# Linear attention and maxout feed-forward on one core: q^T of batch 2 by the DMA crossbar instead of TensorE, batch 3's loads behind it

## Chip, cores and metric

One core of one Trainium2 chip. The metric is the device time of the whole kernel in microseconds (us); the time of a kernel is the median of its runs. Engines are called PE (TensorE), ACT (ScalarE), DVE (VectorE), POOL (GpSimd) and SP (SyncE).

## What is computed

q, k and v have 8 batches, 8 heads, 1024 positions and 64 features. E and F (64 x 1024) shorten k and v along the positions; then a softmax over the 64 shortened positions, and a feed-forward layer with a maximum of two branches. In float32:

```python
k_proj = einsum('ks,bhsd->bhkd', E, k)
v_proj = einsum('ks,bhsd->bhkd', F, v)
scores = matmul(q, k_proj.transpose(0, 1, 3, 2)) / sqrt(64)
attn = softmax(scores)
x = matmul(attn, v_proj)                  # heads side by side: [8192, 512]
out = maximum(x @ w1, x @ w2) @ w_out     # w1, w2: 512 x 1024, w_out: 1024 x 512
```

## The kernel before

Everything runs on one core, with fp16 operands and float32 sums, as one list of steps whose order is written out by hand (`manual_schedule`). Each engine executes its own instructions in the order in which they were written; waits between engines are semaphores, and so are waits for DMAs.

Loads. q, k and v of a batch come in whole, one DMA of 1 MB (fp16) for each tensor, issued from POOL's queue (`load`, L101-105), into tiles of one pool with four buffers (`kvq`, L46): a load waits until the tile of four allocations before it is read. Outputs are stored from SP's queue (`store`, L646-652), from a pool of four buffers (`opool`).

Attention of a batch. `step_kv` (L172) projects k and v, `step_kpt` (L207, on PE) or `step_kpt_dma` (L222, on SP's queue) transposes the projected k, and q has to be transposed too, since the scores contract over the features. There are two ways to do that in the file:

- `step_qt` (L232-245): for four heads and two position blocks, 8 PE transposes of 128 x 128 (L237, matmuls with the identity) into a PSUM bank, then one DVE copy of 128 x 1024 from PSUM into the tile `qt` (L242). Four calls make the q^T of a batch. Batches 0, 1 and 2 use it.
- `step_qt_dma` (L248-252): two DMA transposes from the loaded q tile straight into `qt`, four heads each, issued from SP's queue. Batches 3 to 7 use it.

`step_gate` (L228) is a 1 x 1 copy on POOL that reads the tile named, so that POOL's queue stands still until that tile has been written; the loads of the next batch are written behind it. Batches 3 to 7 have such a gate on `kpt` (L852), and behind it the loads of batch b + 1, as long as there is one.

`step_group` (L333) computes the scores of four heads and half the positions (`score`, L266) and, in the same stretch, the sums and values of the group before (L278). There are four groups to a batch.

Feed-forward. The positions of a batch are cut into two units (batch, half), 16 in all. `up_steps` (L535, matmuls at L554) makes the hidden layer of a unit and `down_steps` (L606, matmuls at L632) its output, both as seven products of half-size blocks, Strassen style, with sums on DVE (L515, L569, L572, L656) and copies on ACT (L525, L604, L700).

Order. The list `slots` (L775-793) strings up the work of unit n: pieces of its down products, with the up products of unit n + 1 between them, in two halves h. Its keys are `("P", n, p, i)` for the pieces of unit 0, `("G", n, h)` for the place where a group of scores goes, `("U", n, h, i)` for up step i. `at_slot` hangs a step behind a key. Batch b's preparation hangs on unit 2b - 3 (L838-853): batch 2 on unit 1, batch 3 on unit 3. For batch 2 the order before is: `step_kv` and the loads of q and v of batch 3 at `("G", 1, 0)`, `step_kpt` at `("U", 1, 0, 1)`, and the four calls of `step_qt` at `("U", 1, 0, 0)`, `("U", 1, 0, 3)`, `("U", 1, 0, 5)` and `("U", 1, 1, 5)`. The first scores of batch 2 stand at `("G", 1, 1)` and use heads 0 to 3; heads 4 to 7 are first read at `("G", 2, 0)`. The load of k of batch 3 stands earlier, with the last `step_qt` of batch 1 (L831).

Which k comes when is decided in `loads` (L756-760): for small b it loads the k of the batch after.

Of the kernel before, what the change touches and what calls it, by code (L numbers as in the profile page):

```python
# [16 lines left out]
def kernel(  # L17
# [14 lines left out]
    B, H, S, D = q.shape  # L32
# [33 lines left out]
    def att_banks(dtype=FP32):  # L66
# [9 lines left out]
            name=nc.get_next_instruction_name(),  # L76
# [20 lines left out]
    def load_all(t, b, n, src):  # L97
        alloc(t, n)
        load(t, n, src, b, 0, H)
# [352 lines left out]
    U = {(b, o): {"n": n, "b": b, "o": o, "t": tiles[b]} for n, (b, o) in enumerate(units)}  # L452
# [260 lines left out]
    t = tiles[0]  # L713
# [41 lines left out]

    def loads(b, *names):  # L756
        for n in names:
            b_ = b + (n == "k" and b < 3)
            if b_ < B:
                load_all(tiles[b_], b_, n, {"k": k, "v": v, "q": q}[n])  # L760

    slots = [
        (0, u0[0]), (None, f(step_at, 0, 1)), (1, u0[1]), (None, f(step_at, 1, 1)),
        (None, lambda: loads(1, "v", "q", "k")),
        (None, wd[1]), (2, u1[0]), (3, u1[1]), (4, u0[2]), (None, wt[0]), (5, u0[3]),
        (None, wd[2]), (None, wt[1]), (6, u1[2]), (7, u1[3]), (8, u0[4]), (9, u0[5]), (None, wd[3]),
# [30 lines left out]
    def at_slot(key, s, *a):  # L797
        steps.setdefault(key, []).append(lambda: s(*a))
# [11 lines left out]
    t = tiles[1]  # L810
    at_slot((0, 19), new_attn, t)
    at_slot((0, 19), lambda: turn.__setitem__(slice(None), [2, 3]))
    for n, x in enumerate((
        "kv", "", "kpt", "qt00 qt10", "", "sc00 qt01 qt11", "sc10", "dn00 in00", "sc01",
        "at00 dn10 in10", "sc11", "at10 dn01 in01", "dn11 in11", "at01", "at11",
    )):
        key = ("P", 0, (n - 1) // 2, (n - 1) % 2) if n else (0, 19)
        for name in x.split():
            if name[0] == "k":
                if name == "kpt":  # L820
                    at_slot(key, step_kpt, t, 0, H, True)
                else:
                    at_slot(key, step_kv, t)
                    at_slot(key, loads, 2, "v", "q")
            else:
                g, j = int(name[2]), int(name[3])
                s_ = {"qt": step_qt, "sc": step_sc,
                      "dn": step_dn, "in": step_inv, "at": step_at}[name[:2]]
                at_slot(key, s_, t, *((4 * g, 4, 2 * j, 2 * j + 2) if name[:2] == "qt" else (g, j)))
                if name == "qt11":  # L830
                    at_slot(key, loads, 2, "k")  # L831
        if n in (1, 5):
            at_slot(key, step_t, 1, (0, 1) if n == 1 else (2, 3))
        if 6 <= n < 10:
            at_slot(key, sums_x, U[0, 1], ((2, 0, 1, 3)[n - 6],))


    t = tiles[2]  # L838
    at_slot(("P", 0, 6, 0), new_attn, t)
    at_slot(("G", 1, 0), step_kv, t, 0, H, "kv", True)  # L840
    at_slot(("G", 1, 0), loads, 3, "q", "v")
    at_slot(("U", 1, 0, 1), step_kpt, t, 0, H, True)
    for i, key in enumerate((("U", 1, 0, 0), ("U", 1, 0, 3), ("U", 1, 0, 5), ("U", 1, 1, 5))):
        at_slot(key, step_qt, t, 4 * (i % 2), 4, i // 2 * 2, i // 2 * 2 + 2, True)
    for b in range(3, B):
        t = tiles[b]
        n = 2 * b - 3
# [8 lines left out]
    for i, (new, old) in enumerate(zip([*groups, none], [none, *groups])):  # L856
        n, h = divmod(i + 3, 2)
# [64 lines left out]
```

## Time and profile before

| | |
|---|---|
| median of 4 runs | 335.63 us (335.35 to 336.16) |
| the profiled execution, its time | 335.29 us |
| its span in the profile | 333.5 us |
| so outside the span | 1.79 us |
| PE busy | 321.5 us (96%) |
| DVE busy | 242.2 us (73%) |
| ACT busy | 201.6 us (60%) |
| granted PE clock, mean | 0.994 |
| unit 1, from its first down piece to its last up step | about 70.3 to 91.6 us in the span |

How to read it: the profile shows one execution, with times in us from the start of its span. A group of instructions is a line of the kernel with its engine, operation and operands, with the busy time, the mean of one, and the idle time of the engine ahead of it. The chain of work that ended last is followed back from the last instruction, at each step to what released it, or else to the instruction before it on its engine: what stands on the chain sets the end of the run, what doesn't stand there lies beside other work. A DMA's time to landing runs from its issue to the semaphore that says its data are there. The time for which an instruction of SP is shown is the time for which it holds SP's queue; the transfer itself goes on after it.

### The profile page before, as it was taken

The numbers are of one execution on the slowest core, as the hardware profiler recorded it, in microseconds if no ns is written. First come the engines' busy times: TensorE is split into PE (matmuls) and PEld (weight loads), VectorE is DVE, ScalarE is ACT, GpSimd is POOL, SyncE is SP. The second block draws the span as 40 slices with busy tenths as digits, with TensorE's granted clock in tenths as the row PEclk, the third lists the DMA queues.
The fourth block names the chain that finished last, engine by engine and source line by source line (L and its number), as shares of the span: only waits on it lengthen the run. The fifth ranks groups of instructions, "written<-read, shape, count | busy, mean of one in ns | idle before, by whom it ended". The sixth has DMA issues, their size and how long they took to land.

```text
span 333.5 us, 9072 instructions
## 1 busy us (share of the span) xinstructions
PE 321.5 (96%) x3884; PEld 249.5 (75%) x3884; DVE 242.2 (73%) x430; ACT 201.6 (60%) x358; POOL 37.1 (11%) x55
## 2 busy tenths in 40 slices
PE   8968999999999999999999999999999999999994
PEld 4533546658888788877888788878887888888883
DVE  1363698988686779677969779677967796969572
ACT  2452421844577677766777577767776777764541
POOL 8655002111000030003000020003000000000000
PEclk9997999999999999999999999999999999999999
DMA  8999999999911969985999889996999321212032
GB/s 155 203 198 205 206 207 182 200 223 211 196 65 48 208 87 210 222 189 88 176 243 214 143 131 231 209 193 91 214 217 202 71 97 33 94 33 96 32 128 94
DMA packets 70520, 52.09 MB, mean 156 GB/s; under 512 B 25296, under 2 KB 70352, under 8 KB 70480
## 3 DMA queue, kind: packets, MB, share of 16 engines
q0 software_dynamic: 29376, 28.31, 53.4%
q1 hardware_dynamic: 41104, 23.21, 28.2%
q8 instruction: 30, 0.49, 0.6%
q14 instruction: 10, 0.08, 0.1%
HBM read 57.15 MB, written 16.78 MB: 222 GB/s over the span
## 4 chain that ended last, share of the span: by engine, by line
PE 84%; DMA 7%; DVE 5%; issue 1%; POOL 1%; ACT 1%; DVEq 0%; POOLq 0%
PE mm_ps L632 41%; PE mm_ps L554 24%; PE mm_ps L400 5%; PE att_ps L180 3%; DMA big<-in_moe_w_dram 3%; PE mm_ps L266 3%; PE att_ps L278 3%; DMA k_sb<-in_k_dram 2%; PE mm_ps L436 2%; DVE xt_sb L325 1%; DMA kpt_sb<-kp_sb 1%; DVE o_sb L656 1%; DVE gt_sb L569 1%; PE mm_ps L278 1%; POOL k_sb L102 1%
## 5 line engine op out<-in xcount | busy, mean ns | idle before, releaser
L525 ACT COPY p_sb<-mm_ps 128x512 f32<-128x512 f32 x172 | 97.3, 593 | 48.2 <-PE mm_ps L554 34.1
L632 PEld LDWEIGHTS <-big 128*128 128x128 f16 x768 | 73.2, 98 | 12.3 <-issue 3.7
L632 PE MATMUL mm_ps<-T_sb,big 128*128 128x256 f16 x576 | 78.1, 273 | 0.0
L569 DVE TENSOR_TENSOR gt_sb<-mm_ps,p_sb 128x512 f16<-128x512 f32 x56 | 38.5, 687 | 46.7 <-PE mm_ps L554 46.7
L554 PE MATMUL mm_ps<-big,big 128*128 128x256 f16 x336 | 50.4, 273 | 0.1
L554 PEld LDWEIGHTS <-big 128*128 128x128 f16 x448 | 43.8, 98 | 5.3 <-issue 0.3
L632 PEld LDWEIGHTS <-gt_sb 128*128 128x128 f16 x384 | 35.5, 98 | 10.1 <-issue 5.8
L632 PE MATMUL mm_ps<-wo_sb,gt_sb 128*128 128x256 f16 x256 | 42.9, 273 | 0.1
L554 PEld LDWEIGHTS <-wd_sb 128*128 128x128 f16 x336 | 32.9, 98 | 4.2 <-issue 0.4
L554 PE MATMUL mm_ps<-xt_sb,wd_sb 128*128 128x256 f16 x224 | 33.6, 273 | 0.2 <-ACT ex_sb L351 0.2
L351 ACT ACTIVATE ex_sb<-mm_ps 128x512 f16<-128x512 f32 x48 | 26.1, 596 | 9.8 <-PE att_ps L278 7.0
L656 DVE TENSOR_TENSOR o_sb<-mm_ps,p_sb 128x512 f32<-128x512 f32 x32 | 21.9, 684 | 10.7 <-PE mm_ps L632 7.2
L377 DVE TENSOR_TENSOR xt_sb<-att_ps,ld_sb 128x1024 f16<-128x1024 f32 x24 | 29.2, 1218 | 0.1
L632 PE MATMUL mm_ps<-m_sb,xt_sb 128*128 128x256 f16 x128 | 24.4, 273 | 0.0
L604 ACT ACTIVATE gt_sb<-mm_ps 128x512 f16<-128x512 f32 x28 | 16.8, 600 | 8.7 <-PE mm_ps L554 8.7
L515 DVE TENSOR_TENSOR big<-gt_sb 128x1024 f16<-128x1024 f16 x32 | 21.9, 684 | 0.2
L572 DVE TENSOR_SCALAR gt_sb<-gt_sb 128x512 f16<-128x512 f16 (+1 forms) x56 | 20.3, 363 | 1.9
L632 PE MATMUL mm_ps<-wo_sb,big 128*128 128x256 f16 x128 | 21.5, 273 | 0.0
L632 PE MATMUL mm_ps<-T_sb,gt_sb 128*128 128x256 f16 x128 | 21.5, 273 | 0.0
L229 POOL COPY junk<-kpt_sb 1x1 f16<-1x1 f16 x5 | 1.2, 235 | 174.2 <-DMA kpt_sb<-kp_sb 174.2
L632 PEld LDWEIGHTS <-xt_sb 128*128 128x128 f16 x192 | 18.8, 98 | 2.2
L400 PE MATMUL mm_ps<-xt_sb,wd_sb 128*128 128x512 f16 x64 | 16.3, 401 | 3.0 <-DVE wd_sb L414 2.1
(87 smaller groups left out, 441.7 us busy)
## 6 DMA issues: line engine op xcount, KB each, us to landing
out_dram<-o_sb SPq DMA_DIRECT2D x63, 256.0 KB, 2.6
k_sb<-in_k_dram POOLq DMA_DIRECT2D x7, 1024.0 KB, 10.5
v_sb<-in_v_dram POOLq DMA_DIRECT2D x7, 1024.0 KB, 17.4
q_sb<-in_q_dram POOLq DMA_DIRECT2D x7, 1024.0 KB, 22.3
k_sb<-in_k_dram POOLq DMA_DIRECT2D x4, 256.0 KB, 6.5
q_sb<-in_q_dram POOLq DMA_DIRECT2D x4, 256.0 KB, 7.6
v_sb<-in_v_dram POOLq DMA_DIRECT2D x2, 512.0 KB, 11.8
big<-in_moe_w_dram POOLq DMA_DIRECT2D x8, 128.0 KB, 10.2
```

Of the source, the lines that this page charges most:

```text
L278: nc.tensor.matmul(out=dst(r ^ (hh % 2))[hh * Z : (hh + 1) * Z, :], lhsT=weights(rows, hh), rhs=ex[rows, hh % 2, hh // 2 * W : (hh // 2 + ...
L351: nc.scalar.activation(out=t["ex", g, j][:, e, :], in_=banks[e], func=ACTF.Exp, scale=scale)
L377: nc.vector.tensor_tensor(out=x_out(t, g, j).rearrange("q z o n -> q o z n"), in0=at_ps.rearrange("q o (z n) -> q o z n", z=2), in1=ld[:, ...
L400: nc.tensor.matmul(out=h_ps, lhsT=wd_sb[:, r, fb * 128 : (fb + 1) * 128], rhs=t["xt"][:, r, :, j * W : (j + 1) * W], start=(r == 0), stop= ...
L515: nc.vector.tensor_tensor(out=S(i), in0=x, in1=y, op=op)
L525: copy(out=x, in_=bank)
L554: nc.tensor.matmul(out=bank[:, m * W : (m + 1) * W], lhsT=w_[:, n_, (2 * d + m) * 128 : (2 * d + m + 1) * 128], rhs=a[:, n_, :], start=(n ...
L569: nc.vector.tensor_tensor(out=c_blk(j, c), in0=two(x), in1=two(y), op=ALU.add)
L572: nc.vector.tensor_scalar_max(ap, ap, 0.0)
L604: nc.scalar.activation(out=out, in_=in_, func=ACTF.Relu)
L632: nc.tensor.matmul(out=bank[:, i * CH : (i + 1) * CH], lhsT=a(c)[:, i * 128 : (i + 1) * 128], rhs=w_(c), start=(n is not None and m == (lo ...
L656: nc.vector.tensor_tensor(out=o_sb, in0=two(x), in1=two(y), op=ALU.add)
```

## The change

In words. The four `step_qt` of batch 2 (32 PE transposes and 4 DVE copies) are left out. Two `step_qt_dma` take their place, both written at `("G", 1, 0)`, behind `step_kv`; so they stand in SP's queue behind the fourth store of unit 0 and ahead of the first store of unit 1. The three loads of batch 3 all move to `("U", 1, 0, 6)`, the end of the first half of unit 1, behind a `step_gate` on `qt`: POOL issues k, v and q of batch 3, in this order, once both transposes have landed. Before, k stood in batch 1's attention, and q and v at `("G", 1, 0)`. The order of PE's, DVE's and SP's other instructions stays as it was, and that of ACT's altogether; POOL has one instruction more.

```diff
     def loads(b, *names):
         for n in names:
-            b_ = b + (n == "k" and b < 3)
+            b_ = b + (n == "k" and b < 2)
...
-                if name == "qt11":
-                    at_slot(key, loads, 2, "k")
...
     t = tiles[2]
     at_slot(("P", 0, 6, 0), new_attn, t)
     at_slot(("G", 1, 0), step_kv, t, 0, H, "kv", True)
-    at_slot(("G", 1, 0), loads, 3, "q", "v")
     at_slot(("U", 1, 0, 1), step_kpt, t, 0, H, True)
-    for i, key in enumerate((("U", 1, 0, 0), ("U", 1, 0, 3), ("U", 1, 0, 5), ("U", 1, 1, 5))):
-        at_slot(key, step_qt, t, 4 * (i % 2), 4, i // 2 * 2, i // 2 * 2 + 2, True)
+    at_slot(("G", 1, 0), step_qt_dma, t, 0, H // 2)
+    at_slot(("G", 1, 0), step_qt_dma, t, H // 2, H)
+    at_slot(("U", 1, 0, 6), step_gate, t, "qt")
+    at_slot(("U", 1, 0, 6), loads, 3, "k", "v", "q")
```

## Prediction

> **What bounds the kernel now.** I read the page's busy times first, then the chain of waits, then the waits of PE, then single tiles and queues.
>
> ```profile
> PE 321.5 (96%) x3884; PEld 249.5 (75%) x3884; DVE 242.2 (73%) x430; ACT 201.6 (60%) x358; POOL 37.1 (11%) x55
> ...
> PE 84%; DMA 7%; DVE 5%; issue 1%; POOL 1%; ACT 1%; DVEq 0%; POOLq 0%
> ```
>
> PE carries 84% of the chain that ended last. A busy PE alone would prove little, so what counts is where PE stands still. The waits of PE between 70 and 120 us, the stretch of the change, are these:
>
> ```profile
> PE mm_ps L278 <- DVE xt_sb L325: 0.3, 1, 0.3
> PE mm_ps L554 <- ACT ex_sb L351: 0.2, 1, 0.2
> ```
>
> So 0.5 us in 50: PE is the bound there, and a PE instruction that goes takes its time out of the run, unless a wait grows. The chain through unit 1 shows the instructions in question (start, us, what):
>
> ```profile
> 77.37 0.60 DVE qt_sb L242
> 77.97 0.61 DVE gt_sb L569
> 78.58 0.04 issue
> 78.62 0.60 PE mm_ps L554 x4
> 79.22 0.45 PE att_ps L237 x8
> ...
> 81.41 0.45 PE att_ps L237 x8
> ...
> 83.60 0.39 PE mm_ps L266 x16
> ...
> 89.63 0.45 PE att_ps L237 x8
> ```
>
> Three of the four groups of transposes (L237) stand on the chain themselves; at the fourth, at 75.27 us, the chain runs for a moment over DVE instead, where it meets a copy that serves these transposes (L242). The first scores of batch 2 (L266) follow at 83.5.
>
> What a DMA transpose costs here is seen at batch 3, which has it already. SP's queue from 106 us on (start, us in the queue), and the DMA issues between 108 and 112 us and of the load of batch 2's q at 54.4 us with their median time to landing:
>
> ```profile
> 108.53 5.62 SPq L249 DMA_TRANSPOSE qt_sb<-q_sb  x2
> ```
>
> ```profile
> qt_sb<-q_sb SPq DMA_TRANSPOSE x1, 6.1
> ```
>
> ```profile
> q_sb<-in_q_dram POOLq DMA_DIRECT2D x1, 1024.0 KB, 15.6
> ```
>
> The pair holds SP for 5.62 us. The first half lands 6.1 us after issue, the second 5.7 us after its own issue, which follows 2.0 us after the first: both are there about 7.8 us after the start.
>
> **What the Trainium skill says.** (1) "Perfetto Trace Analysis", section "Identifying the Most-Contended Engine": busy time of matmuls is a poor measure, because they are pipelined. The trace agrees: one transpose is shown with 219 ns, but eight of them take up 0.44 us of the stream (L237 starts at 79.06, the next product at 79.50). I cost by starts, not by busy time. (2) "VectorE: DVE Perf Modes", section "The three transpose paths": 390 ns for 128 x 128 on TensorE, 1309 ns on the crossbar. Back to back it is 55 ns here on PE, so the trace disagrees for a stream, and decides. (3) "Advanced Engine Details and Errata", section "X-Bar Transpose (TRN2)": crossbar transposes run at 350 to 400 GB/s, and only one stream of them may be in flight. Both halves come from SP, so they are one stream. A half is 512 KB, which gives an estimate of 1.3 to 1.5 us; the 6.1 us measured are used instead. (4) "DMA: Bandwidth & Descriptors", section "Issuing engines are not separate DMA queues": all transfers share 16 engines and interleave. The trace agrees: the three stores of 68 to 70 us, beside loads, took 7.7 to 8.0 us to land, the one at 108 us, beside none, 2.5 us.
>
> **The change part by part.**
>
> *Removed from PE:* 4 groups of 8 transposes, each 0.44 us by starts (75.27 to 75.71, 79.06 to 79.50, 81.25 to 81.69, 89.47 to 89.92): 4 x 0.44 = 1.75 us. All are on PE's stream, which has no room, so all of it comes off the path, if PE's neighbours keep up.
>
> *Do they keep up?* Before the score at 83.5 three groups go, so ACT's and DVE's results are wanted up to 1.3 us sooner. The tightest is the product at 78.62, which waits for a DVE sum (L569). PE would have been there at 78.53, so 0.09 us is lost before. After the change PE is there at 78.09. DVE's copy at 77.29 (L242, 0.60 us of the stream) goes too, so the sum starts at 77.29 instead of 77.89 and ends at about 77.98; with 0.04 us of signalling, 78.02. It is in time by 0.07 us, and the 0.09 us are won as well. The ACT copies that later products wait for are themselves fed by PE and move with it: the product at 82.13 waits for the copy of 80.58 (ends 81.17), and comes 1.41 us sooner, at 80.72, while the copy, 0.97 us sooner, ends at 80.20. The wait of 0.18 us behind ACT's exponential (L351) stays.
>
> *Removed from DVE:* 4 copies of 0.68 us, 2.7 us. Except for the one just counted they lie beside PE work: nothing. Without that cover (DVE the bound) they would be up to 2.7 us of gain, which PE's missing waits exclude.
>
> *Added to SP:* two transposes. They stand behind the store of L700, issued at 69.64 for 0.37 us, so from 70.0 on, and wait for q of batch 2: 54.43 + 15.6 = 70.03. So issue at about 70.1, first half landed at 70.1 + 6.1 = 76.2, second at 77.9. The scores want heads 0 to 3 at 83.53 - 1.40 = 82.1: cover 5.9 us. Heads 4 to 7 are wanted at 91.8 - 1.8 = 90.0: cover 12 us. SP is held to 75.7; the next store comes at 76.46 before (about 76 after), so nothing waits behind them. If that cover went, stores would queue, and DVE stops only when four output buffers are full. Cost: nothing. The bounds are below.
>
> *Moved on POOL:* three loads, from 59.75, 73.87 and 75.03, to behind the gate. The gate opens at 77.9; with 0.5 us for it and 0.9 us for each issue (118.68 to 120.91 for batch 4's) the loads start at 78.4, 79.3 and 80.2. Batch 4's triple took 10.5, 17.7 and 22.3 us to land, so k lands at 88.9, v at 97.0, q at 102.5. Batch 3's transposes are due on SP at 108.53 - 1.84 = 106.7, its projection at 111.68 - 1.84 = 109.8: cover 4.2 us and more. Behind the gate on POOL stands nothing but these loads until the next gate at 118.7. Cost: nothing. Without cover each us of lateness passes on, less 1.2 us that SP has free before kpt's transpose (114.15 to about 115.3) and 0.7 us that kpt has before its score.
>
> *Given back to DMA:* k of batch 3 no longer runs from 59.75 to 77.2, so stores and q of batch 2 land rather sooner. No PE wait there names a DMA: nothing.
>
> *What is next late:* after the change nothing new; at 155 us PE waits 0.5 us for kpt of batch 4, a DMA that took 3.9 us instead of the 2.7 of the other four. I leave it in; if it falls out by chance, 0.5 us more is won.
>
> *The cost that before does not show:* a transpose in unit 1. From below: zero, if it lands by 82.1, and a gain is excluded because the PE and DVE shares are counted above. From above: stores beside loads took 3.2 times as long (7.9 against 2.5); stretched so, 6.1 becomes 19.5, landing at 89.6, a wait of 7.5 us. I take zero: batch 3's pair, behind three stores as well, met the same load, and all loads ahead have landed by 70.1.
>
> *Sum:* 1.75 + 0.09 = 1.84 us. Span 333.5 - 1.84 = 331.66; with the 1.79 us outside the span 333.45, against 335.29 of that execution. The median of the runs is 0.34 us above it, so 335.63 - 1.84 = 333.8.
>
> **The rivals.**
>
> *A, as worked out,* 333.8 (chance 0.80).
>
> *B, DVE or ACT becomes the bound in unit 1* and part of the gain stays there. For it: only 0.07 us of slack at 78.09, and DVE is 1.9 of 2 us busy between 76 and 80. Against: three of the four DVE copies that go lie before 84 us as well, so DVE's work shrinks where PE's does. If half the gain is lost, 335.63 - 0.9 = 334.7 (0.08).
>
> *C, slower: the first half of q^T comes late at the scores* (first weight load of L266 in unit 1). It decides from a landing at 82.1, and the run is slower than before once it is past 82.1 + 1.84 = 84.0, which is 13.9 us from issue, 2.3 times batch 3's 6.1. For it: stores issued at 68 to 70 us took up to 8.0 us, and the transposes are in the same queue; should they start only when the last store is in (69.64 + 7.9 = 77.5), they land at 83.6, a wait of 1.5, 335.3. At the full stretch of 3.2 it is 335.63 + 7.5 - 1.84 = 341.3. Against: those stores ran beside k of batch 3, which the gate holds back. Past the break-even I price it at a landing of 85.3 (a stretch of 2.5): a wait of 3.2, 335.63 + 3.2 - 1.84 = 337.0 (0.07).
>
> *D, nothing changes:* the gain is eaten by a wait of about C's size or by batch 3's loads landing after 108.6 (28 us from issue, where 22 to 24 were seen), 335.6 (0.05). That the change doesn't do what it says is excluded by the order of the instructions: 32 transposes and 4 copies are gone.
>
> **How the numbers follow.** What a measurement of this kernel can tell from no change is about 0.2%, 0.67 us. A and B end faster than 334.96 in nearly all cases: 0.80 and 0.07 of 0.08. Within 0.2%: the other 0.01 of B and D's 0.05, 0.06. Slower: C, 0.07. The range takes A with the chance wait at 155 us gone (333.8 - 0.5 = 333.3, less 0.2 for the spread of the runs, 333.1), and B to its end, 335.0. It leaves out C and D, 0.12, and tails of A.
>
> **What would show it.** Right: no L237 after 60 us; the first scores of batch 2 at about 82.1 with no wait for a DMA; the pair on SP at about 70, landed by 78; the product of 78.62 at 78.1; POOL's loads at 78 to 81, q landed by 104; L249 of batch 3 at 106.7 without a wait for a load. Wrong: a wait of L266 for `qt`, a wait of L554 for DVE at 78 us of more than 0.1 us, L249 of batch 3 released by the load of q.

## The result and the profile after

The changed kernel takes 333.92 us (median of 33 runs, 331.39 to 337.55), the kernel before 335.84 us in the same sittings (median of 52, 333.82 to 338.46). The two medians differ by 1.92 us. The ratio, which leaves out runs in a slower state with a lower granted clock (one of the 33) and is not the quotient of the medians, is 0.9933, 95% interval 0.9919 to 0.9947: faster by 2.25 us, at least 1.8 and at most 2.7. Forecast were 1.84 us and 333.8 us.

The profiled executions differ by far less: spans of 333.1 and 333.5 us. The reason lies ahead of the change. Up to 53 us the two programs are the same, yet unit 0 begins 1.27 us later in the profile of after (first projection product of batch 1 at 52.63 instead of 51.36 us); in the profiles of the twelve experiments below the projection of batch 2 begins anywhere between 70.66 and 72.94. So I measure inside a profile, with two rulers that begin at the same instruction, the first projection product of batch 2 (71.66 before, 72.92 after): the short one ends at the first scores of batch 2 (83.53 and 83.30), the long one at the first scores of batch 3 (119.14 and 118.40). These are the three instructions, before and then after (start, us, what):

```profile
71.66 0.40 PE L180 MATMUL att_ps<-k_sb,eft 128*64 128x512 f16 x1
83.53 0.41 PE L266 MATMUL mm_ps<-qt_sb,kpt_sb 64*32 64x256 f16 x16
119.14 0.62 PE L266 MATMUL mm_ps<-qt_sb,kpt_sb 64*32 64x256 f16 x16
```

```profile
72.92 0.40 PE L180 MATMUL att_ps<-k_sb,eft 128*64 128x512 f16 x1
83.30 0.41 PE L266 MATMUL mm_ps<-qt_sb,kpt_sb 64*32 64x256 f16 x16
118.40 0.62 PE L266 MATMUL mm_ps<-qt_sb,kpt_sb 64*32 64x256 f16 x16
```

| | before | after | difference |
|---|---|---|---|
| short ruler, us | 11.87 | 10.38 | -1.49 |
| long ruler, us | 47.48 | 45.48 | -2.00 |

The page of after, busy times and shares of the chain:

```profile
PE 321.3 (96%) x3852; PEld 248.3 (75%) x3852; DVE 239.7 (72%) x426; ACT 201.3 (60%) x358; POOL 37.1 (11%) x56
...
PE 90%; DVE 6%; DMA 1%; issue 1%; ACT 0%; DVEq 0%; SPq 0%
```

PE has 32 matmuls fewer (3852 for 3884), but its busy time falls by only 0.2 us. The second profile of the same kernel (the first experiment) has 319.8 us, so busy time differs too much from one execution to the next to read the gain from it. The waits of PE between 48 and 125 us in after:

```profile
PE mm_ps L278 <- DVE xt_sb L325: 0.6, 2, 0.3
PE mm_ps L554 <- ACT ex_sb L351: 0.2, 1, 0.2
```

The kernel before has the same two lines in this window; no wait for a DMA has come in. The chain through unit 1 (start, us, what) no longer leaves PE:

```profile
78.47 0.44 PE mm_ps L554 x4
78.91 0.44 PE mm_ps L632 x4
79.35 0.53 PE mm_ps L554 x4
79.88 0.44 PE mm_ps L632 x4
...
83.37 0.39 PE mm_ps L266 x16
```

Before, a piece of DVE stood here, with four groups L237 after it or beside it. Now a group of four products takes 0.44 us each, and 0.53 at one place: a rest of 0.09 us, which is looked at below. SP's queue and POOL's in after, and the DMA issues that answer to those shown of batch 3 before:

```profile
71.39 5.09 SPq L249 DMA_TRANSPOSE qt_sb<-q_sb  x2
```

```profile
79.28 0.32 POOL L229 COPY junk<-qt_sb 1x1 f16<-1x1 f16 x1 [22.69 <-DMA qt_sb<-q_sb]
79.79 0.87 POOL L102 DMA_DIRECT2D k_sb<-in_k_dram  x1 [0.20 <-issue]
80.65 0.88 POOL L102 DMA_DIRECT2D v_sb<-in_v_dram  x1
81.52 0.90 POOL L102 DMA_DIRECT2D q_sb<-in_q_dram  x1
```

```profile
qt_sb<-q_sb SPq DMA_TRANSPOSE x1, 5.4
```

```profile
q_sb<-in_q_dram POOLq DMA_DIRECT2D x1, 1024.0 KB, 22.2
```

The first half lands at 71.39 + 5.4 = 76.8, 6.5 us before the scores; q of batch 3 lands at 103.7, and SP takes up batch 3's transposes at 107.79. Both covers held: 6.5 us where 5.9 were forecast, and 4.1 us where 4.2 were. One wait grew: PE waits 0.9 us for a kpt, at 225 us (batch 6), where before it waited 0.5 us at 155 us (batch 4). In these two executions that costs 0.4 us of the gain, and the last experiment is about it. The sum of the profiles: +1.26 (start) - 2.00 (long ruler) + 0.4 (kpt) = -0.34 us; the spans differ by -0.4.

### The profile page after: what moved, and what is told of

The parts are those of the page before. It is cut to its first block, busy times and chain, and to the rows that moved or that the text cites. A ratio compares the mean times of both kernels' runs of the same rounds, so it can differ in the third digit from the quotient of the medians.

```text
span 333.1 us, 9012 instructions
## 1 busy us (share of the span) xinstructions
PE 321.3 (96%) x3852; PEld 248.3 (75%) x3852; DVE 239.7 (72%) x426; ACT 201.3 (60%) x358; POOL 37.1 (11%) x56
## 4 chain that ended last, share of the span: by engine, by line
PE 90%; DVE 6%; DMA 1%; issue 1%; ACT 0%; DVEq 0%; SPq 0%
PE mm_ps L632 42%; PE mm_ps L554 24%; PE mm_ps L400 4%; PE att_ps L180 3%; PE att_ps L278 3%; PE mm_ps L266 3%; PE mm_ps L140 3%; PE mm_ps L436 2%; PE mm_ps L180 2%; DVE xt_sb L325 2%; DMA kpt_sb<-kp_sb 1%; DVE o_sb L656 1%; PE mm_ps L278 1%; PE mm_ps L237 1%; DVE qt_sb L242 1%
## 5 line engine op out<-in xcount | busy, mean ns | idle before, releaser
L569 DVE TENSOR_TENSOR gt_sb<-mm_ps,p_sb 128x512 f16<-128x512 f32 x56 | 38.5, 688 | 47.6 <-PE mm_ps L554 47.6
L515 DVE TENSOR_TENSOR big<-gt_sb 128x1024 f16<-128x1024 f16 x32 | 21.9, 684 | 0.2
L569 DVE TENSOR_TENSOR gt_sb<-p_sb 128x512 f16<-128x512 f32 x28 | 19.1, 680 | 0.0
```

Source lines behind the costliest of these rows:

```text
L515: nc.vector.tensor_tensor(out=S(i), in0=x, in1=y, op=op)
L569: nc.vector.tensor_tensor(out=c_blk(j, c), in0=two(x), in1=two(y), op=ALU.add)
```

## Experiments

Theory: the gain is the time of PE's stream in unit 1, and the DMA side costs nothing because both covers hold. Rivals: part of the gain comes from the loads of batch 3 moved out of the way; DVE is the bound at 78 us; the covers are smaller than they look. All rulers in one table, times as medians and as ratio to the kernel before in the same sitting:

| kernel | short ruler | long ruler | time, us | ratio (95%) |
|---|---|---|---|---|
| before | 11.87 | 47.48 | 335.84 | 1 |
| changed | 10.38 | 45.48 | 333.92 | 0.9933 (0.9919 to 0.9947) |
| changed, again | 10.39 | 45.49 | 333.87 | 0.9937 (0.9919 to 0.9954) |
| loads only | 11.87 | 47.47 | 336.03 | 1.0000 (0.9983 to 1.0017) |
| PE back | 11.62 | 47.17 | 335.31 | 0.9985 (0.9970 to 1.0000) |
| PE and DVE back | 11.87 | 47.48 | 335.66 | 0.9992 (0.9974 to 1.0010) |
| no gate | 11.72 | 52.25 | 345.38 | 1.0252 (1.0200 to 1.0304) |
| k early | 10.38 | 45.48 | 333.50 | 0.9933 (0.9916 to 0.9950) |
| late | 10.39 | 48.57 | 337.24 | 1.0042 (1.0021 to 1.0062) |
| late, k early | 10.39 | 45.49 | 333.93 | 0.9948 (0.9925 to 0.9970) |
| kpt by DMA | 10.70 | 46.00 | 334.03 | 0.9943 (0.9922 to 0.9963) |
| kpt, sums moved | 10.17 | 45.41 | 332.73 | 0.9904 (0.9872 to 0.9935) |
| kpt, sums turned | 9.82 | 44.98 | 332.69 | 0.9902 (0.9881 to 0.9923) |
| fetch shifted | 10.38 | 45.48 | 332.48 | 0.9909 (0.9880 to 0.9938) |

**The changed kernel again,** beside three others on one chip.

> The changed kernel once more, as the base for the three kernels beside it: ruler 45.5, ratio to before 0.993.

As expected. The rulers repeat to 0.01 us, so differences of 0.1 us in them can be read, though the times of whole runs spread over nearly 4 us (331.35 to 335.16 us without the longest).

**Loads only.** The kernel before with the three loads of batch 3 moved; the gate stands on kpt, which PE and DVE still make.

```diff
-            b_ = b + (n == "k" and b < 3)
+            b_ = b + (n == "k" and b < 2)
...
-                if name == "qt11":
-                    at_slot(key, loads, 2, "k")
...
-    at_slot(("G", 1, 0), loads, 3, "q", "v")
...
+    at_slot(("U", 1, 0, 6), step_gate, t)
+    at_slot(("U", 1, 0, 6), loads, 3, "k", "v", "q")
```

> The kernel before with the loads of batch 3 alone moved: k, v and q behind a gate on kpt at the end of unit 1's first half; q^T of batch 2 stays on PE. If the gain is PE's stream alone: ruler 47.5, time as before within 0.2%. If part of the gain comes from k of batch 3 being out of the way between 60 and 77 us: ruler shorter, or the stretch from unit 0 to unit 1 shorter, by 0.2 us or more, and a time up to 0.5 us under before.

Both rulers and the time are those of before. Moving the loads neither gains nor costs: that rival falls.

**PE back, and PE and DVE back.** The changed kernel with batch 2's 32 PE transposes at their old places, into a PSUM bank that nobody reads; then with four DVE copies from there into a spare tile as well. q^T still comes by DMA.

```diff
+    def step_spare(t, h0, i0):
+        qt_ps = att_banks(FP16)[:, 0, :]
+        for h in range(4):
+            for i in range(2):
+                nc.tensor.transpose(
+                    out=qt_ps[:, (h * 2 + i) * 128 : (h * 2 + i + 1) * 128],
+                    in_=t["q"][:, h0 + h, 2 * (i0 + i) : 2 * (i0 + i) + 2, :],
+                    identity=ident16,
+                )
...
+    for i, key in enumerate((("U", 1, 0, 0), ("U", 1, 0, 3), ("U", 1, 0, 5), ("U", 1, 1, 5))):
+        at_slot(key, step_spare, t, 4 * (i % 2), i // 2 * 2)
```

> The changed kernel with the 32 PE transposes of batch 2 put back at their old places into a PSUM bank that nobody reads (no DVE copies); q^T still comes by DMA. If PE's stream carries the gain: ruler 45.48 + 1.75 less the 0.09 us wait for DVE that is then covered, 47.1 to 47.2, and a time 1.7 us over the changed kernel. If the gain came from DVE or from the loads: ruler near 45.5.

> As the kernel with the PE transposes put back, and their four DVE copies too, into a spare tile. Leaves the DMA transposes and the moved loads as the only difference from before. If these cost nothing: ruler 47.5 and a time as before within 0.2%; the step from the kernel without the copies is what DVE's copies cost, 0.2 to 0.3 us. If the DMA side costs or gains by itself, the ruler is off 47.5 by that.

PE's part alone puts the long ruler from 45.48 to 47.17, +1.69 us; the copies add 0.31, and the ruler is that of before to 0.01. So the gain in the ruler splits into 1.69 us of PE and 0.31 us of DVE (taken in this order; why the 1.69 are not 1.75 is told below), and there the DMA transposes with their moved loads cost nothing. Of the 0.31 us, 0.25 lie in the short ruler; there the product of 78.62 in the kernel before starts 0.69 us after its predecessor instead of 0.44, and in the changed kernel it still starts 0.53 us after it (PE's timeline before, then after):

```profile
77.93 0.60 PE L632 MATMUL mm_ps<-T_sb,big 128*128 128x256 f16 x4
78.62 0.60 PE L554 MATMUL mm_ps<-big,big 128*128 128x256 f16 x4
```

```profile
78.75 0.60 PE L632 MATMUL mm_ps<-T_sb,big 128*128 128x256 f16 x4
79.28 0.60 PE L554 MATMUL mm_ps<-big,big 128*128 128x256 f16 x4
```

The 0.60 us in the second column are no price: where nothing waits, the next product starts 0.44 us after.

**No gate.** The changed kernel without the line `step_gate`; POOL then issues k of batch 3 at 61.0 us and v and q at 75.1 and 76.3, as soon as their buffers are free.

```diff
-    at_slot(("U", 1, 0, 6), step_gate, t, "qt")
```

> The changed kernel without the gate: the transposes of batch 2 stay on SP, but k of batch 3 is issued at about 60 us again and v and q of batch 3 at about 75 us, so that the transposes run beside loads. Ruler: from the first projection product of batch 2 to the first scores of batch 3 (47.48 us before, 45.48 us in the changed kernel). If the gate is only caution: the first half lands within 12 us of its issue, ruler 45.5, time as the changed kernel. If transposes stretch beside loads as the stores did (3.2 times, 5.4 to 17 us), the scores of batch 2 wait some 5 us, ruler 51, time about 339.

The transposes do stretch. The first half takes 13.2 us to land (between 71 and 72 us), 2.4 times the 5.4, and PE's waits between 60 and 120 us are these:

```profile
qt_sb<-q_sb SPq DMA_TRANSPOSE x1, 13.2
```

```profile
PE mm_ps L266 <- DMA qt_sb<-q_sb: 5.3, 2, 4.0
PE mm_ps L278 <- DVE xt_sb L325: 0.6, 2, 0.3
```

5.3 us in two waits, 1.3 for the first half and 4.0 for the second, which took 18.4 us to land. But the long ruler grew by 6.8 us. Where is the rest? In the clock, after the long wait (engine columns PE, PEld, DVE, ACT, POOL, then the granted PE clock, DMA share, GB/s):

```profile
92.00:96.00 4.00, 0.48 (x5) 0.18 (x2) 2.43 (x6) 0.29 (x1) 0.00 (x0) 1.00 1.22 213
96.00:98.00 2.00, 1.52 (x42) 0.92 (x43) 0.00 (x0) 0.84 (x2) 0.00 (x0) 0.50 1.09 381
98.00:100.00 2.00, 2.00 (x14) 1.51 (x13) 0.00 (x0) 1.32 (x3) 0.00 (x0) 0.64 0.30 100
100.00:102.00 2.00, 2.00 (x20) 1.79 (x19) 0.99 (x3) 1.33 (x3) 0.00 (x0) 1.00 0.00 0
```

PE comes back at half speed, until about 99.4 us, and the next group of scores comes 9.56 us after the one that waited, instead of 8.20: 1.4 us lost after the wait. The wait of 1.3 us had no such sequel. The profiled run, at 340.69 us, was the fastest of this kernel's six; the other five took 345.3 to 348.5, with a mean granted clock of 0.972 to 0.985 where the profiled run had 0.989. Where they lost beyond it was not traced.

**k early.** As the changed kernel, but k of batch 3 is loaded where it was before; only v and q wait behind the gate.

```diff
-            b_ = b + (n == "k" and b < 2)
+            b_ = b + (n == "k" and b < 3)
...
+                if name == "qt11":
+                    at_slot(key, loads, 2, "k")
...
-    at_slot(("U", 1, 0, 6), loads, 3, "k", "v", "q")
+    at_slot(("U", 1, 0, 6), loads, 3, "v", "q")
```

> The changed kernel with k of batch 3 loaded at its old place (about 60 us), only v and q behind the gate; the transposes at 71.4 us run beside the tail of that load, which landed at 77 us. If a transpose stretches only while a load is in flight: the first half takes 8 to 10 us instead of 5.4, the cover of 12 us from issue holds, no wait, ruler 45.5, time as the changed kernel. If k alone did the harm of the ungated run: first half at 13 us, a wait of 1 us or more.

The first half took 9.4 us beside the tail of that load, from 69.1 to 78.5 us, and the scores came at 81.0: the cover held, and nothing changes. So it is v and q of batch 3 that have to wait for the transposes; k need not have been moved.

**Late, and late with k early.** The two transposes one store later in SP's queue, with all three loads behind the gate, then with k loaded early as above.

```diff
-    at_slot(("G", 1, 0), step_qt_dma, t, 0, H // 2)
-    at_slot(("G", 1, 0), step_qt_dma, t, H // 2, H)
+    at_slot(("U", 1, 0, 3), step_qt_dma, t, 0, H // 2)
+    at_slot(("U", 1, 0, 3), step_qt_dma, t, H // 2, H)
```

> The changed kernel with the two transposes one store later in SP's queue, behind the first store of unit 1 (issued at 77.7 us): issue at about 78.2 instead of 71.4. With a landing of 5.4 us the first half is in at 83.6, the scores want it at 83.3: a wait of 0.2 to 0.8 us, ruler 45.7 to 46.3, all of it passed on to the time. If there were more slack than the prediction counts: ruler 45.5 and no wait. The loads behind the gate start some 7 us later as well and q of batch 3 lands at about 110.5, after the 107 us where SP wants it: if that counts, L249 of batch 3 waits 3 us, and the scores of batch 3 wait 1 to 2 us more.

> k of batch 3 early, v and q behind the gate, and the transposes one store later in SP's queue (issue at about 77 to 78 us, when k has landed). If the late kernel lost by the third load behind the gate landing too late (q at 111.7 where SP wanted it at 106.5): with only two loads behind the gate q lands some 16 us after issue instead of 23.7, at 103, no wait at the scores of batch 3, ruler 45.5 to 46, time within 0.5 us of the changed kernel. If lateness of the transposes themselves did it: a wait of 2 to 3 us at the scores of batch 3 and the half clock after it again.

In the first, SP issues at 76.90, the first half lands 5.1 us later, at 82.00, and the scores start at 82.00: the cover used to its end, and no wait yet (short ruler 10.39). The loss comes 38 us later. The waits of SP's queue between 100 and 120 us, then those of PE between 40 and 150:

```profile
SPq L249 <- DMA q_sb<-in_q_dram: 4.9, 1, 4.9
```

```profile
PE mm_ps L266 <- DMA kpt_sb<-kp_sb: 2.9, 1, 2.9
```

The loads behind the gate start at 86.3, q of batch 3 is the third and lands 23.7 us after its issue at 88.0, batch 3's transposes wait 4.9 us for it, kpt of batch 3 stands behind them in SP's queue, and the scores of batch 3 wait 2.9 us for kpt. The prediction's slack fits: of 4.9 us it takes off 1.2 that SP has free and 0.7 that kpt has, which leaves 3.0. Then the clock again:

```profile
116.00:120.00 4.00, 1.29 (x32) 0.74 (x30) 2.29 (x5) 1.18 (x2) 0.00 (x0) 0.91 0.96 203
120.00:122.00 2.00, 1.82 (x23) 1.05 (x24) 0.00 (x0) 1.12 (x3) 1.39 (x3) 0.50 0.00 0
122.00:124.00 2.00, 2.00 (x11) 1.45 (x10) 0.00 (x0) 0.94 (x2) 1.42 (x2) 0.50 0.83 64
124.00:126.00 2.00, 2.00 (x11) 1.44 (x10) 0.00 (x0) 1.22 (x3) 0.00 (x0) 0.50 1.13 167
126.00:130.00 4.00, 4.00 (x38) 3.56 (x36) 3.78 (x7) 1.76 (x3) 0.00 (x0) 0.98 1.22 200
```

The clock falls during the wait, at about 119.3 us, and stays at a half until about 126.1, six us of it with PE at work: from the scores of batch 3 to the next group 11.14 us instead of 8.52, 2.6 us on top of the 2.9. That isn't the price in every execution. The profiled one took 339.22 us at a mean granted clock of 0.985. Of this kernel's 20 runs ten had a mean clock of 0.993 or more and took 335.0 to 337.8 us; the other ten had 0.990 or less and took 337.0 to 340.4. So the loss through the clock seems not to come every time; no run of the first ten was traced. With k early, q lands 17.0 us after its issue at 87.8, at 104.8, no DMA is waited for, and ruler and time are those of the changed kernel. So this lateness of the transposes did no harm by itself; with the third load behind the gate it did.

**kpt of batch 2 by DMA,** to take more from PE: as in batches 3 to 7, projection with `dma=True` and no `step_kpt`. Then two DVE sums of unit 1 moved behind the DVE add that held PE up, then their order turned.

```diff
     at_slot(("P", 0, 6, 0), new_attn, t)
-    at_slot(("G", 1, 0), step_kv, t, 0, H, "kv", True)
-    at_slot(("U", 1, 0, 1), step_kpt, t, 0, H, True)
     at_slot(("G", 1, 0), step_qt_dma, t, 0, H // 2)
     at_slot(("G", 1, 0), step_qt_dma, t, H // 2, H)
+    at_slot(("G", 1, 0), step_kv, t, 0, H, "kv", True, True)
-    at_slot(("U", 1, 0, 6), step_gate, t, "qt")
+    at_slot(("U", 1, 0, 6), step_gate, t)
```

```diff
-            where = (("P", 1, 0, 2), 0), (("P", 1, 1, 0), 1), (("P", 1, 1, 2), 2), (("U", 1, 0, 1), 3)
+            where = (("P", 1, 0, 2), 0), (("P", 1, 1, 0), 1), (("U", 1, 0, 1), 2), (("U", 1, 0, 1), 3)
...
-            for key, i in (end, 0), (("P", n, 0, 0), 1), (("P", n, 1, m), 2), (("P", n, 2, m), 3):
+            for key, i in (end, 0), (("P", n, 0, 0), 1), (("U", 1, 0, 1) if n == 1 else ("P", n, 1, m), 2), (("P", n, 2, m), 3):
```

In the third, `("P", 1, 2, 1)` stands in place of the last `("U", 1, 0, 1)`.

> The changed kernel with kpt of batch 2 by DMA too, as batches 3 to 7 have it: 16 PE transposes of 64 x 64 (0.37 us by starts) and a DVE copy of 128x512 go, a DVE copy of 64x512 and one DMA transpose on SP behind the two of q^T come; the gate waits for kpt. If PE's stream carries the time: ruler 45.1, time 0.4 us under the changed kernel. If kpt comes late behind the transposes of q^T (both held SP until 76.5 us): L266 waits for kpt, ruler above 45.5.

> kpt of batch 2 by DMA as in the run before, and two DVE sums of unit 1 (the third sum of x for unit 2, 0.33 us by starts, and the third sum of g for unit 1, 0.60 us) moved behind the DVE add for which PE waited 0.88 us by starts in that run. If DVE's order was what ate that gain: no wait at that add, ruler 45.48 - 0.37 - 0.09 = 45.0, time 0.4 to 0.5 us under the changed kernel. If something else came of the DMA of kpt: ruler stays at 46.0.

> As the kernel with kpt of batch 2 by DMA and two sums moved, with the order of these two turned: the sum of x for unit 2, for which PE waited 0.35 us by starts in that run, now comes ahead of the sum of g. If DVE's order is all that is left: no wait of PE for DVE in unit 1, ruler 45.4 - 0.35 = 45.1, time 0.4 us under the changed kernel. If the sum of g is then the late one: a wait at the down product that reads it, ruler 45.4.

kpt by DMA alone takes 0.37 us from PE and loses 0.32 us in the short ruler. PE's timeline and DVE's in unit 1 of that kernel:

```profile
77.88 0.60 PE L632 MATMUL mm_ps<-T_sb,big 128*128 128x256 f16 x4
79.20 0.60 PE L554 MATMUL mm_ps<-big,big 128*128 128x256 f16 x4 [0.72 <-DVE gt_sb L569]
```

```profile
77.53 0.68 DVE L515 TENSOR_TENSOR big<-gt_sb 128x1024 f16<-128x1024 f16 x1
78.13 0.42 DVE L515 TENSOR_TENSOR big<-xt_sb 128x512 f16<-128x512 f16 x1
78.47 0.68 DVE L569 TENSOR_TENSOR gt_sb<-mm_ps,p_sb 128x512 f16<-128x512 f32 x1
```

PE comes at 77.88 + 0.44 = 78.32 and waits till 79.20, 0.88 us: here DVE is the bound. Counted from the first projection product the sum (L569) starts 0.33 us later than in the changed kernel, and the extra kp copy on DVE, which stands ahead of it, takes 0.32 us from start to start. With the two L515 moved behind L569 the short ruler falls to 10.17; the product now waits 0.2 us for a sum, at 78.98. With their order turned that wait is gone too: 9.82, which is 0.56 under the changed kernel (0.37 of the 16 transposes, 0.09 of the wait that the changed kernel still had, and 0.09 at the product ahead of the transposes, which takes 0.53 us from start to start in the changed kernel and 0.44 here); of it 0.50 remain in the long ruler. So the rival "DVE is the bound at 78 us" is true from there on. This kernel takes 332.69 us. Its interval overlaps that of the changed kernel, so the 1 us between the two medians isn't settled by the times, the 0.5 us in the ruler is.

**Fetch shifted.** The wait for kpt at batch 4 before, at batch 6 after. The DMA views of before (151 to 156 us) and after (222 to 226 us) show the same company:

```profile
q8 instruction: 1, 0.02, 1.7%
...
kpt_sb<-kp_sb SPq DMA_TRANSPOSE x1, 3.9
```

```profile
q8 instruction: 1, 0.02, 1.6%
...
kpt_sb<-kp_sb SPq DMA_TRANSPOSE x1, 4.2
```

One transfer of 16 KB on the queue for instructions falls 1.15 us (before) and 2.15 us (after) after the issue of that kpt, and of the five kpts in each profile only that one lands late, 3.9 and 4.2 us for the usual 2.7. The page of before counts 30 such transfers, and PE has two times 3884 instructions there (weight loads and matmuls): about one transfer for 259 of them. To try it, 32 small matmuls, 64 instructions, were added where PE waits for its first weights.

```diff
     step_wd(0)
+    w_ps = mm_bank(n=turn[0])
+    for _ in range(32):
+        nc.tensor.matmul(
+            out=w_ps[:, 0:32], lhsT=ones16[:, 0:128], rhs=ones16[:, 0:32], start=True, stop=True
+        )
```

> The changed kernel with 32 small matmuls (32 columns, into a PSUM bank that is overwritten) added where PE waits 2.1 us for the first weights anyway, at about 24 us: they cost nothing there, but every later PE instruction stands 64 instructions further on in PE's list, as in the kernel before. In five traces a transfer of 16 KB on queue 8 (instructions) fell 1 to 2 us after the issue of one DMA transpose of kpt and that transpose landed about a microsecond late: at batch 4 in the kernel before and the three kernels with PE's 64 instructions back or never gone, at batch 6 in the changed kernel. If these transfers fetch PE's instructions and so sit where the count of instructions puts them: the late kpt goes back to batch 4, with a wait of 0.4 to 0.5 us, instead of 0.9 us at batch 6; ruler 45.5; time up to 0.5 us under the changed kernel. If the place has another reason: batch 6 and 0.9 us again.

The wait between 140 and 170 us in that kernel:

```profile
PE mm_ps L266 <- DMA kpt_sb<-kp_sb: 0.6, 1, 0.6
```

The late kpt is back at batch 4 (a 16 KB transfer 1.14 us after its issue), with 0.6 us; batch 6 lands in time, and the long ruler is 45.48 as it should be. So the count of PE's instructions puts the transfer near one kpt or another. Whether it hits is a matter of tenths of a us: no gate, and late with k early, have the changed kernel's count, but there the transfer falls 2.25 and 2.80 us after the kpt of batch 6, which lands in the usual 2.7 us, and nothing waits; late has it at 2.20 us, and waits 0.9 us. The three kernels with kpt of batch 2 by DMA have 32 PE instructions fewer again, and there it falls 0.85 to 1.0 us after the kpt of batch 3, which takes 3.2 to 3.4 us. The time, 332.48 us, is 1.4 us under the changed kernel's, of which the wait explains 0.3; the intervals overlap.

## Why the prediction was right, step by step

*PE's four groups, 1.75 us:* right. Without rounding each takes 0.447 us from start to start, 1.79 in all. Putting them back alone cost 1.69 us in the long ruler, since they cover the 0.09 us again that the changed kernel waits for DVE: 1.79 - 0.09 = 1.70.

*DVE at 78 us, 0.09 us won and in time by 0.07 us:* right in kind, wrong in size, and the sum was not in time. I took the loss from the chain (78.53 to 78.62), where the product ahead was shown until 78.53. But its 0.60 us overlap the next product by 0.16; by starts PE had come at 77.93 + 0.44 = 78.37 and lost 0.25 us. In after the add still comes 0.09 us late, so 0.16 us were won, not 0.09. The prediction says that it costs by starts, and for this one term it did not. With 1.79 and 0.16 the ruler's 2.00 are there but for 0.05 us, which lie behind the first scores of batch 2. The run with the DVE copies back has 0.06 us there too, so "nothing" for the other copies is a little too low; which of them it is was not traced.

*SP and the landing of q^T, nothing:* right. Issue at 71.39 is 70.1 with the 1.3 us of the late start taken off; 5.4 us to landing for the 6.1 taken. The late kernel shows that the cover ends where it was put: landing at 82.00, scores at 82.00. *Rival C,* a stretch beside loads, is what happens without the gate, but not where it was priced. The first half landed 13.2 us after its issue, under the break-even of 13.9, and its wait of 1.3 us alone would have left part of the gain. The loss came from the second half, for which C had no price: 18.4 us to landing, a wait of 4.0, and 1.4 through the clock.

*Loads behind the gate, nothing:* right; q of batch 3 had 4.1 us to spare, 4.2 were forecast. What the prediction left out is part of the price of failing: "each us of lateness passes on". In the profile of the late kernel 2.9 us of waiting cost 2.6 us more through the clock. The Trainium skill has this, in "TensorE: Matmul & The Clock Gate", section "Why this matters for your kernels": idle gaps of PE over about 3 us bring half the clock back. Here gaps of 2.9 and 4.0 us did, and one of 1.3 us did not. But the figure is no safe limit: near 25 us, where PE waits 2.1 us for its first weights (1.2 us in fetch shifted) after some shorter waits, the clock falls to 0.50 for some 3.4 us in the kernel before, in the changed one and in all others but k early (6.8 us in kpt by DMA).

*kpt at 155 us, "if it falls out by chance":* it was not chance alone. The change itself moved it, since 64 PE instructions fewer shift the transfers of instructions, and in the profiles 0.4 us of the gain went there: 2.00 - 0.4 = 1.6 us, under the 1.92 of the medians and the 2.25 (1.8 to 2.7) of the ratio. What the remaining few tenths are was not found in the traces; each kernel has one profile, the changed one two.

That 1.84 us stand so close to the measured gain is in part luck: the stretch of the change gave 2.00, the moved wait took 0.4, and 0.3 us or more that nobody forecast made up for it.

## What to carry to other kernels

Where one engine carries the chain, price a removed instruction by the distance between starts, and look next at the engine whose result it waits for: the next 0.37 us taken from PE were worth nothing until two sums on DVE had moved out of the way. A DMA transpose belongs in a stretch without loads, or needs a cover for the 13 to 18 us that its halves took here beside three loads, and what is gated behind it has a due time of its own: the third of three loads decided. A missed cover can cost more than its wait: after waits of 2.9 and 4.0 us PE lost 2.6 and 1.4 us more through its clock, in the two executions that were traced.

## What the runs showed of the hardware

- In the late kernel the granted clock was 0.50 for some 6.8 us, from within a wait of PE of 2.9 us (119.3 to 126.1 us); without the gate it was 0.50 for some 3.4 us at the end of a wait of 4.0 us (96.0 to 99.4). This cost 2.6 and 1.4 us on top of the waits. After a wait of 1.3 us it stayed at 1.00. Behind PE's wait near 25 us (2.1 us, or 1.2 in fetch shifted, with shorter ones ahead of it) it was 0.50 for 3.4 us, in kpt by DMA for 6.8; only in k early, with the same wait of 2.1 us, it stayed at 1.00. So the length of one wait doesn't decide alone; what else does is not shown.
- A DMA transpose of 512 KB took 4.3 to 6.9 us with no load in flight (all batches and kernels), 9.4 us beside the tail of one load, and 13.2 and 18.4 us for the two halves beside the three loads without the gate.
- When a transfer of 16 KB on the instruction queue fell 1.1 to 2.2 us after the issue of a DMA transpose of kpt, that transpose landed 1.0 to 1.7 us late (3.7 to 4.4 us for 2.7); at 2.25 and 2.80 us it landed in time. Removing or adding 64 PE instructions moved the hit from one batch to another.
